# Causal attention, then a cosine MLP, on one core: other PSUM banks and another order for a few instructions

## The chip, the cores and the metric

One core of a Trainium2 chip. The core's engines are TensorE (PE; PEld is its weight load), VectorE (DVE), ScalarE (ACT), GpSimd (POOL) and SyncE (SP), which issues transfers. Each runs its own instructions in order and waits for the others by semaphores. PSUM has 8 banks, numbered 0 to 7 here. The metric is the device time of one execution in microseconds (us), the median of the runs.

## What is computed

Attention over 4 batches and 12 heads, 448 rows of 64, then an MLP of 768 to 2048 to 768 over 1792 tokens:

```python
scores = scale * np.matmul(q, k.transpose(0, 1, 3, 2))
scores = np.where(mask, -1000000000.0, scores)      # causal
attn = softmax(scores)
x = np.matmul(attn, v)        # laid out as 1792 tokens x 768
h = x @ w_in
out = (h * np.cos(h)) @ w_out
```

Inputs are float32; the two weight matrices come as float64 and are converted in the kernel.

## The kernel before

The order of all instructions is the order in which the code is written (a manual schedule); nothing reorders it. The program has two parts.

**Attention** (`attention`, the loop at L497) goes over N = 24 pairs of heads (4 batches by 6), one pair per step i, and works on several pairs at once, in a pipeline of steps. The 448 rows of a pair are three blocks of 128 and an end of 64; the causal mask leaves block rows 0, 1 and 2 ("top" is row 2, 384 wide; "low" are rows 0 and 1) and the end rows, which are done for two pairs together in odd steps. In step i:

- TensorE computes the scores of pair i (L336: top into banks 4 and 5, low into banks 6 and 7, the two heads j = 0 and 1 in one bank each), in odd steps the end scores of pairs i - 1 and i (L348, into banks 2 and 3), transposes the next pair's Q (L304, L307, bank 1), transposes the probabilities of pair i - 1 in three groups (`tp_top`, `tp_first`, `tp_last`, all at L422), transposes the next K (L304, bank 1 again), the end probabilities of pair i - 2 (`tp_ends`, L442), and forms P V of pair i - 3 (`av`, L457, bank 0).
- DVE masks the scores and takes the row maximum while it moves them out of PSUM (L357), forms the reciprocals of the sums (`inverse`, L389 and L390), copies the groups `tp_top` and `tp_first` out of PSUM (L311), and finishes P V (L479).
- ACT does the exponentials with their sums (L376) and the other copies out of PSUM (L313: Q, K, `tp_last`, and the ends in `evac_ends`), and the first half of finishing P V (L475).
- POOL multiplies the probabilities by the reciprocals (L396: low rows 0 and 1, ends, top), which must be done before they are transposed.

Between steps a piece of the MLP's first weights is converted (`convert_weight`: L128, L131, L137, L141 on DVE, L134, L142, L143 on POOL). Which bank a group of transposes uses is set in each step by the tuple `tb`:

```python
tb = (4, (TA_BANK, 6)[i % 2], 5, (6, 7)[i % 2])   # top, first, last, ends; TA_BANK = 2
```

so in even steps `tp_first` uses bank 2 and `tp_ends` bank 6, in odd steps 6 and 7. The next step's scores need banks 4 to 7 again, and its end scores banks 2 and 3. In steps N and N + 1 the first matmuls of the MLP (L589 to L591) fill TensorE's time (`fill`, banks 1 and 6).

**MLP** (`moe`) goes through slots k; each forms 2 x 18 matmuls of the first layer (L589 to L591, banks 4 and 5), the cosine of the result (`cosine_stages`: L597, L601, L602 on ACT, L599, L604 on DVE), and four chunks of the second layer for the slot before (`m2a_chunk`, L685, bank pairs 6-7 and 0-1 in turn), which DVE adds to the sums (L673). Between these the weights of later slots are converted: `mask` (L151, L153, L155 on ACT), `pack` (L162, L166, L170 on DVE), `halve` (L706 on ACT, L707 on POOL). `some(gen, n)` issues the next n stages of such a sequence, `run(gen)` the rest. The slots' code is `slot` at L879.

Of the kernel before, what the change touches and what calls it, by code (L numbers as in the profile page):

```python
# [21 lines left out]
def kernel(  # L22
# [19 lines left out]
    P = 128  # L42
# [55 lines left out]
    def f32(ap):  # L98
        return ap.bitcast(F32)
# [113 lines left out]
    def attention(filler_of):  # L213
        with (
# [94 lines left out]
            def evac(dst, src, dve=False):  # L309
                if dve:  # L310
                    nc.vector.tensor_copy(dst, src)  # L311
                else:
                    nc.scalar.copy(dst, src)  # L313

            def evac_qk(i, which, dve=False, n=W):
                d, s = qkt[i, which]
                evac(d[:, 0:n], s[:, 0:n], dve)
# [63 lines left out]
            def exp_block(i, c, j):  # L381
                exp(prob[i][:, j, OFF[c] : OFF[c] + (c + 1) * P], stats[i], col(c, j))
# [4 lines left out]
            def inverse(i, lo, up):  # L387
                st = stats[i]
                nc.vector.tensor_scalar(st[:, 2, lo:up], st[:, 1, lo:up], 1e-9, None, op0=ALU.add)  # L389
                nc.vector.reciprocal(st[:, 2, lo:up], st[:, 2, lo:up])  # L390
# [55 lines left out]
            def evac_ends(i, b):  # L446
# [2 lines left out]
                    banks8[:, b].rearrange("p (k h t) -> p k h t", k=NB + 1, h=2),  # L449
                )  # L450

            def av(i):
                vn, vt = vals.pop(i)
                o = banks8[:, O]
                for kc in range(NB + 1):
                    for j in range(2):
                        nc.tensor.matmul(  # L457
                            o[heads(j), kc * P : S],
                            lhsT=(vn[:, kc] if kc < NB else vt)[:, heads(j)],
                            rhs=ptr[i][:, j ^ i % 2, kc * (KS + P) : kc * KS + S],  # L460
                            start=(kc == 0), stop=(kc == NB),
                        )
                return o

            def x_of(i):
                b, hp = pairs[i]
# [5 lines left out]

            def finish_hi(i):
                for hi, _, cs in x_of(i):
                    nc.scalar.copy(hi, banks8[:, O, cs])  # L475

            def finish_lo(i):
                for hi, lo, cs in x_of(i):
                    nc.vector.tensor_tensor(lo, banks8[:, O, cs], f32(hi), op=ALU.subtract)  # L479

            extra = []

# [14 lines left out]
            for i in range(N + 4):  # L497
                cur, prev, nxt = i < N, 0 < i <= N, i + 1 < N
                ends_of, old, done = 0 <= i - 2 < N, 0 <= i - 3 < N, 0 <= i - 4 < N
                tb = (4, (TA_BANK, 6)[i % 2], 5, (6, 7)[i % 2])  # L500
                if i + 2 < N:
                    load_qk(i + 2)
                if prev:
                    load_v(i - 1)
                if i <= N:
                    open_stat(i)
                if cur:
                    open_scores(i)
                    scores_main(i, TOP, SC[0:2])
                    scores_main(i, LOW, SC[2:4])  # L510
                    if i % 2:
                        scores_ends(i - 1)
                if i == 0:
                    transpose_ends(0, O)
                    transpose_main(1, 1, TB_BANK)
                    transpose_main(1, 0, QK)
                    transpose_ends(1, QK)
                elif nxt:
                    transpose_main(i + 1, 0, QK)
                    transpose_ends(i + 1, QK)  # L520
                if done:
                    finish_hi(i - 4)
                if i == 1:
                    for j in range(2):
                        masked_block(i, 2, j, 0, SC[j])
                if 0 < i <= N + 1:
                    inverse(i - 1, 0 if prev else TAIL_COL, TAIL_COL + (i > 1))
                if prev:
                    normalise_block(i - 1, 0)
                    normalise_block(i - 1, 1)  # L530
                if ends_of:
                    normalise_ends(i - 2)
                if cur:
                    for j in range(2):
                        if i != 1:
                            masked_block(i, 2, j, 0, SC[j])
                        exp_block(i, 2, j)
                        if i and nxt and j == i % 2:
                            evac_qk(i + 1, 0, n=W + P)
                    if i == 0:  # L540
                        evac(qkt[0, 0][0][:, W : W + P], banks8[:, O, W : W + P])
                    masked_block(i, 0, 0, 0, SC[2])
                    if i == 0:
                        evac_qk(1, 1, dve=True)
                        evac_qk(1, 0, n=W + P)
                    masked_block(i, 1, 0, P, SC[2])
                if done:
                    finish_lo(i - 4)
                if cur:
                    inverse(i, TOP_COL, TOP_COL + 2)  # L550
                    normalise_block(i, 2)
                    masked_block(i, 0, 1, 0, SC[3])
                    masked_block(i, 1, 1, P, SC[3])
                    exp_block(i, 0, 0)
                    exp_block(i, 1, 0)
                if prev:
                    masked_ends(i - 1)
                if i in (N, N + 1):
                    fill((14, 12)[i - N])
                if prev:  # L560
                    open_ptr(i - 1)
                    tp_top(i - 1, tb[0])
                    tp_first(i - 1, tb[1])
                if prev:
                    tp_last(i - 1, tb[2])
                if nxt and i:
                    transpose_main(i + 1, 1, QK)
                    evac_qk(i + 1, 1)
                if cur:
                    exp_block(i, 0, 1)  # L570
                    exp_block(i, 1, 1)
                if prev:
                    exp_ends(i - 1)
                if ends_of:
                    tp_ends(i - 2, tb[3])
                    evac_ends(i - 2, tb[3])
                if i == N + 2:
                    run(extra[0])
                if old:
                    av(i - 3)  # L580
                yield i
# [71 lines left out]
    def some(gen, k=1):  # L653
        for _ in range(k):
            next(gen, None)

    def moe(ring, early, firsts):
        pend = None
        with tc.tile_pool(name="mo", bufs=1) as mo:
# [219 lines left out]
            def slot(g, t0, n, k, prev, first):  # L879
# [36 lines left out]
                if k in (2, 3):  # L916
                    run(pack(ia, mo))
                    some(firsts)
                    c0 = cosine_stages(hv[0], n)
                    some(c0, 2)  # L920
                    x_side(k - 3)
                    mb = mask(ib)
                    if k == 2:
                        some(mb)
                        some(c0)
                        side_out()
                    else:
                        some(c0)
                        some(mb)
                    some(mb)  # L930
                    (r0,) = c0
                    run(mb)
                    last_side()
                    ta = halve(ia)
                    run(m1_sum(ring, g, 1, t0, n, hv[1]))
                    pb = pack(ib, mo)
                    some(pb)
                    c1 = cosine_stages(hv[1], n)
                    some(c1)
                    if k == 2:  # L940
                        side_out()
                    gs.append(split(r0, *g_tiles(n)))
                    m2a_chunk(*prev, 0)
                    if k == 2:
                        some(c1)
                        some(pb)
                        some(c1)
                        m2a_chunk(*prev, 1)
                        run(pb)
                        tb = halve(ib)  # L950
                    else:
                        run(pb)
                        m2a_chunk(*prev, 1)
                        tb = halve(ib)
                        some(c1, 2)
                    if k == 2:
                        side_out()
                    mc = mask(ic)
                    some(mc)
                    (r1,) = c1  # L960
                    gs.append(split(r1, *g_tiles(n)))
                    if k == 3:
                        first_side(2, ta, tb)
                    m2a_chunk(*prev, 2)
                    run(mc)
                    m2a_chunk(*prev, 3)
                    if k == 2:
                        side_out()
                    store_side()
                    return gs  # L970
# [455 lines left out]
```

## Time and profile before

| what | value |
|---|---|
| median of 3 runs | 626.55 us (626.45 to 626.62) |
| profiled execution | 627.32 us, span 625.5 us |
| TensorE busy | 609.8 us (97% of the span) |
| DVE, ACT, POOL busy | 476.1, 419.5, 449.3 us |
| granted TensorE clock | 0.999 of full speed |
| moved by DMA | 133.27 MB, 212 GB/s over the span |

The attention takes about the first 180 us. Busy time of one engine says little by itself; what counts is who ends last at each place, which the waits and the order in time tell. A row of the order in time gives the start, the duration, the engine, the line and operation, the tiles with the number of instructions (x), and in brackets the idle time of the engine ahead of it and what ended it. A row of several instructions covers them from the first start to the last end. TensorE's matmuls overlap and their ends are modelled, so its idle time is better taken from start to start.

### The profile page before, as it was taken

Reading aid. Unit: us, or ns where it says so; the run is one execution under the profiler, and the core shown is the slowest. Engines: PE = TensorE matmul, PEld = TensorE weight load, DVE = VectorE, ACT = ScalarE, POOL = GpSimd, SP = SyncE. Lnnn points to the kernel's source line nnn. Section 1 sums busy time; section 2 is a strip of 40 time slices with the busy share of each in tenths; the row PEclk is TensorE's granted clock in tenths of the full one; section 3 lists DMA queues with packets and bytes.
Section 4 is the critical chain, followed back from the end, with each engine's and each line's share of the span. In section 5 each row is a group of like instructions: output and inputs, shape, how many; then the busy total and the mean of one; then the engine's idle time right before and its main releaser. Section 6 shows DMA issues by size and latency. Waiting matters only on the chain.

```text
span 625.5 us, 11531 instructions
## 1 busy us (share of the span) xinstructions
PE 609.8 (97%) x3825; PEld 537.2 (86%) x3825; DVE 476.1 (76%) x1023; ACT 419.5 (67%) x928; POOL 449.3 (72%) x456
## 2 busy tenths in 40 slices
PE   8799999999999999999999999999999999999996
PEld 6577667677669988999999999999999999999995
DVE  6788888888838678878777777764368887887886
ACT  5889988989766769877777777743335544644540
POOL 3676677677624968887877787772588788888885
PEclk9999999999999999999999999999999999999999
DMA  7656457563405776968696979669997568549104
GB/s 179 148 121 166 115 131 176 135 171 93 135 8 175 241 286 228 360 214 329 225 334 208 327 233 341 209 249 377 401 399 256 176 210 281 195 153 326 55 1 151
DMA packets 124042, 133.27 MB, mean 213 GB/s; under 512 B 72112, under 2 KB 108320, under 8 KB 123984
## 3 DMA queue, kind: packets, MB, share of 16 engines
q1 hardware_dynamic: 116384, 106.23, 53.8%
q0 software_dynamic: 4928, 24.78, 10.8%
q10 hardware_dynamic: 2672, 1.54, 0.8%
q8 instruction: 30, 0.49, 0.3%
q14 instruction: 28, 0.23, 0.1%
HBM read 82.58 MB, written 49.94 MB: 212 GB/s over the span
## 4 chain that ended last, share of the span: by engine, by line
PE 59%; DVE 2%; ACT 1%; issue 0%; DVEq 0%; ACTq 0%
PE banks L685 17%; PE banks L1113 12%; PE banks L1133 12%; PE banks L590 5%; PE banks L591 5%; PE banks L589 5%; PE banks L1037 2%; PE banks L1150 2%; DVE ct L170 0%; DVE acc L1160 0%; DVE banks L166 0%; DVE banks L162 0%; DVE r L599 0%; DVE acc L673 0%; DVE sct L770 0%
## 5 line engine op out<-in xcount | busy, mean ns | idle before, releaser
L673 DVE TENSOR_TENSOR acc<-acc,banks 128x768 f32<-128x768 f32 (+1 forms) x122 | 112.6, 932 | 43.2 <-PE banks L685 32.8
L685 PE MATMUL banks<-w,gh 128*128 128x384 f32 x512 | 109.8, 335 | 0.6 <-DVE acc L673 0.6
L685 PEld LDWEIGHTS banks<-w,gh 128*128 128x128 f32 x512 | 90.8, 188 | 2.4 <-DVE acc L673 1.3
L396 POOL TENSOR_TENSOR pb<-pb,stat 128x768 f32<-128x768 f32 (+2 forms) x72 | 74.0, 1042 | 24.9 <-DVE stat L390 10.1
L376 ACT ACTIVATE pb<-pb,stat 128x384 f32<-128x384 f32 (+1 forms) x144 | 72.1, 504 | 13.4 <-DVE stat L357 13.4
L591 PE MATMUL banks<-xa,w 128*128 128x512 f32 x192 | 75.2, 392 | 0.0
L590 PE MATMUL banks<-xa,w 128*128 128x512 f32 x192 | 75.0, 391 | 0.0
L589 PE MATMUL banks<-xa,w 128*128 128x512 f32 x192 | 74.9, 390 | 0.0
L707 POOL TENSOR_TENSOR w<-ct,w 128x768 fp32r<-128x768 f32 x28 | 51.9, 1854 | 19.0 <-PE banks L685 7.8
L685 PE MATMUL banks<-w,gl 128*128 128x384 f32 x256 | 65.1, 335 | 0.0
L357 DVE CUSTOM_DVE_ANT_0 pb<-banks,mask 128x384 f32<-128x384 f32 (+1 forms) x144 | 53.9, 418 | 7.9 <-PE banks L336 7.6
L597 ACT ACTIVATE ni<-banks 128x512 int32<-128x512 f32 (+1 forms) x64 | 34.5, 539 | 36.6 <-PE banks L591 22.7
L616 POOL TENSOR_TENSOR gl<-r,gh 128x512 fp32r<-128x512 f32 x32 | 41.5, 1300 | 20.4 <-ACT gh L615 20.2
L599 DVE SCALAR_TENSOR_TENSOR r<-ni,banks 128x512 f32<-128x512 int32 (+1 forms) x56 | 35.1, 626 | 21.5 <-ACT ni L597 21.0
L601 ACT ACTIVATE r<-r 128x512 f32<-128x512 f32 (+1 forms) x56 | 32.8, 586 | 23.0 <-DVE r L599 22.5
L336 PE MATMUL banks<-flat 64*128 64x256 f32 (+2 forms) x288 | 40.7, 402 | 6.2 <-ACT pm L313 3.2
L685 PEld LDWEIGHTS banks<-w,gl 128*128 128x128 f32 x256 | 46.4, 188 | 0.0
L604 DVE SCALAR_TENSOR_TENSOR r<-r,banks 128x512 f32<-128x512 f32 (+1 forms) x56 | 35.1, 626 | 14.0 <-ACT r L602 13.9
L1113 PE MATMUL banks<-xb,bb 128*128 128x384 f32 x234 | 44.7, 334 | 0.0
L457 PE MATMUL banks<-pm,vn 128*64 128x192 f32 (+2 forms) x288 | 44.1, 441 | 0.7 <-DVE xb L479 0.7
L1133 PE MATMUL banks<-big,gh 128*128 128x384 f32 x168 | 42.6, 334 | 0.0
L591 PEld LDWEIGHTS banks<-xa,w 128*128 128x128 f32 x192 | 36.0, 188 | 7.6
(149 smaller groups left out, 1528.2 us busy)
## 6 DMA issues: line engine op xcount, KB each, us to landing
bb<-w_in_d SPq DMA_DIRECT2D x48, 384.0 KB, 5.5
land<-in_moe_w_in_dram SPq DMA_DIRECT2D x14, 768.0 KB, 5.5
land<-in_moe_w_out_dram SPq DMA_DIRECT2D x14, 768.0 KB, 5.8
w_out_d<-w POOLq DMA_DIRECT2D x14, 768.0 KB, 5.2
big<-w_out_d SPq DMA_DIRECT2D x25, 384.0 KB, 4.0
w_in_d<-w POOLq DMA_DIRECT2D x7, 768.0 KB, 3.9
raw_d<-ct POOLq DMA_DIRECT2D x14, 384.0 KB, 7.8
land<-in_q_dram SPq DMA_DIRECT2D x48, 96.0 KB, 3.1
```

The costliest lines, as they stand in the source:

```text
L357: nc.vector.tensor_tensor_reduce(out=dst, in0=src, in1=m, scale=-scale, scalar=3.0e38, op0=ALU.add, op1=ALU.min, accum_out=st[:, 0, n : n ...
L376: nc.scalar.activation(dst, dst, AF.Exp, scale=-1.0, bias=st[:, 0, n : n + 1], accum_out=st[:, 1, n : n + 1],)
L396: nc.gpsimd.tensor_tensor(dst, dst, r.to_broadcast(list(dst.shape)), op=ALU.mult)
L457: nc.tensor.matmul(o[heads(j), kc * P : S], lhsT=(vn[:, kc] if kc < NB else vt)[:, heads(j)], rhs=ptr[i][:, j ^ i % 2, kc * (KS + P) : kc ...
L589: yield nc.tensor.matmul(hv, lhsT=wh[:, f], rhs=x[:, 0, cc, t], start=(cc == 0), stop=False)
L590: yield nc.tensor.matmul(hv, lhsT=wh[:, f], rhs=x[:, 1, cc, t], start=False, stop=False)
L591: yield nc.tensor.matmul(hv, lhsT=wl[:, f], rhs=x[:, 0, cc, t], start=False, stop=(cc == NCC - 1))
L673: nc.vector.tensor_tensor(d, d, o, op=ALU.subtract)
L685: nc.tensor.matmul(o[:, e, 0:EH], lhsT=a[:, cs], rhs=w[:, e * EH : (e + 1) * EH], start=(x == 0), stop=(x == 5),)
L707: nc.gpsimd.tensor_tensor(w[:, 1], tf, f32(w[:, 0]), op=ALU.subtract)
L1113: nc.tensor.matmul(o, lhsT=w[:, u, k * P : (k + 1) * P], rhs=x[k][:, v], start=k + m == 0, stop=k == K - 1 and m == 2,)
L1133: nc.tensor.matmul(o[:, b % 2, 0:EH], lhsT=g_ops[i][u][:, c * P : (c + 1) * P], rhs=wouts[g, i][:, v], start=(x == 0), stop=(x == 2),)
```

## The change

Five edits; no instruction is added or taken away.

1. Banks and order of the transposes: `tp_top` in bank 4, then `tp_last` in 5, then `tp_first` in 6, in every step; `tp_ends` in bank 2 in even steps, 7 in odd ones.
2. In every step the reciprocal of the top sums (`inverse` of 2 columns) and the top normalisation behind it come after the low masked rows of the second head instead of before.
3. Steps 0 to 2: in step 0 the copy of the next Q moves between the two top exponentials; in step 1 the transposes and the copy of the next K move ahead of two exponentials and of `tp_last` and `tp_first`; in step 2 the top masked rows move ahead of the reciprocals, as in step 1.
4. P V of the last pair goes to bank 7 instead of bank 0.
5. In slot 3 the first mask stage comes ahead of the cosine's ACT stages, and one more `pack` stage ahead of the first chunk.

```diff
--- before.py
+++ after.py
@@ -449,9 +449,12 @@
                     banks8[:, b].rearrange("p (k h t) -> p k h t", k=NB + 1, h=2),
                 )
 
+            def o_of(i):
+                return banks8[:, 7 if i == N - 1 else O]
+
             def av(i):
                 vn, vt = vals.pop(i)
-                o = banks8[:, O]
+                o = o_of(i)
                 for kc in range(NB + 1):
                     for j in range(2):
                         nc.tensor.matmul(
@@ -460,7 +463,6 @@
                             rhs=ptr[i][:, j ^ i % 2, kc * (KS + P) : kc * KS + S],
                             start=(kc == 0), stop=(kc == NB),
                         )
-                return o
 
             def x_of(i):
                 b, hp = pairs[i]
@@ -472,11 +474,11 @@
 
             def finish_hi(i):
                 for hi, _, cs in x_of(i):
-                    nc.scalar.copy(hi, banks8[:, O, cs])
+                    nc.scalar.copy(hi, o_of(i)[:, cs])
 
             def finish_lo(i):
                 for hi, lo, cs in x_of(i):
-                    nc.vector.tensor_tensor(lo, banks8[:, O, cs], f32(hi), op=ALU.subtract)
+                    nc.vector.tensor_tensor(lo, o_of(i)[:, cs], f32(hi), op=ALU.subtract)
 
             extra = []
 
@@ -497,7 +499,7 @@
             for i in range(N + 4):
                 cur, prev, nxt = i < N, 0 < i <= N, i + 1 < N
                 ends_of, old, done = 0 <= i - 2 < N, 0 <= i - 3 < N, 0 <= i - 4 < N
-                tb = (4, (TA_BANK, 6)[i % 2], 5, (6, 7)[i % 2])
+                e_bank = (TA_BANK, 7)[i % 2]
                 if i + 2 < N:
                     load_qk(i + 2)
                 if prev:
@@ -520,7 +522,7 @@
                     transpose_ends(i + 1, QK)
                 if done:
                     finish_hi(i - 4)
-                if i == 1:
+                if i in (1, 2):
                     for j in range(2):
                         masked_block(i, 2, j, 0, SC[j])
                 if 0 < i <= N + 1:
@@ -532,38 +534,42 @@
                     normalise_ends(i - 2)
                 if cur:
                     for j in range(2):
-                        if i != 1:
+                        if i not in (1, 2):
                             masked_block(i, 2, j, 0, SC[j])
                         exp_block(i, 2, j)
-                        if i and nxt and j == i % 2:
+                        if nxt and j == i % 2:
                             evac_qk(i + 1, 0, n=W + P)
-                    if i == 0:
-                        evac(qkt[0, 0][0][:, W : W + P], banks8[:, O, W : W + P])
                     masked_block(i, 0, 0, 0, SC[2])
                     if i == 0:
                         evac_qk(1, 1, dve=True)
-                        evac_qk(1, 0, n=W + P)
+                        evac(qkt[0, 0][0][:, W : W + P], banks8[:, O, W : W + P])
                     masked_block(i, 1, 0, P, SC[2])
                 if done:
                     finish_lo(i - 4)
                 if cur:
+                    masked_block(i, 0, 1, 0, SC[3])
+                    masked_block(i, 1, 1, P, SC[3])
                     inverse(i, TOP_COL, TOP_COL + 2)
                     normalise_block(i, 2)
-                    masked_block(i, 0, 1, 0, SC[3])
-                    masked_block(i, 1, 1, P, SC[3])
-                    exp_block(i, 0, 0)
-                    exp_block(i, 1, 0)
+                    if i != 1:
+                        exp_block(i, 0, 0)
+                        exp_block(i, 1, 0)
                 if prev:
                     masked_ends(i - 1)
                 if i in (N, N + 1):
                     fill((14, 12)[i - N])
                 if prev:
                     open_ptr(i - 1)
-                    tp_top(i - 1, tb[0])
-                    tp_first(i - 1, tb[1])
+                    tp_top(i - 1, 4)
+                if i == 1:
+                    transpose_main(i + 1, 1, QK)
+                    evac_qk(i + 1, 1)
+                    exp_block(i, 0, 0)
+                    exp_block(i, 1, 0)
                 if prev:
-                    tp_last(i - 1, tb[2])
-                if nxt and i:
+                    tp_last(i - 1, 5)
+                    tp_first(i - 1, 6)
+                if nxt and i > 1:
                     transpose_main(i + 1, 1, QK)
                     evac_qk(i + 1, 1)
                 if cur:
@@ -572,8 +578,8 @@
                 if prev:
                     exp_ends(i - 1)
                 if ends_of:
-                    tp_ends(i - 2, tb[3])
-                    evac_ends(i - 2, tb[3])
+                    tp_ends(i - 2, e_bank)
+                    evac_ends(i - 2, e_bank)
                 if i == N + 2:
                     run(extra[0])
                 if old:
@@ -920,13 +926,10 @@
                     some(c0, 2)
                     x_side(k - 3)
                     mb = mask(ib)
+                    some(mb)
+                    some(c0)
                     if k == 2:
-                        some(mb)
-                        some(c0)
                         side_out()
-                    else:
-                        some(c0)
-                        some(mb)
                     some(mb)
                     (r0,) = c0
                     run(mb)
@@ -940,6 +943,8 @@
                     if k == 2:
                         side_out()
                     gs.append(split(r0, *g_tiles(n)))
+                    if k == 3:
+                        some(pb)
                     m2a_chunk(*prev, 0)
                     if k == 2:
                         some(c1)
```

Banks don't show in an instruction's row below, which names all of PSUM `banks`. Three places in the order of the instructions show the rest.

DVE, the middle of step 5 (`xa<-banks,xa` finishes P V of an earlier pair; `pb` are probabilities, `stat` the sums), before:

```order
L479 TENSOR_TENSOR xa<-banks,xa 128x448
L389 TENSOR_SCALAR stat<-stat 128x2
L390 RECIPROCAL stat<-stat 128x2
L357 ISA pb,stat<-banks,mask 128x128
L357 ISA stat 128x1
L357 ISA pb,stat<-banks,mask 128x256
L357 ISA stat 128x1
L357 ISA pl_94,stat<-banks,mask_t 128x448
```

and now:

```order
L481 TENSOR_TENSOR xa<-banks,xa 128x448
L357 ISA pb,stat<-banks,mask 128x128
L357 ISA stat 128x1
L357 ISA pb,stat<-banks,mask 128x256
L357 ISA stat 128x1
L389 TENSOR_SCALAR stat<-stat 128x2
L390 RECIPROCAL stat<-stat 128x2
L357 ISA pl_94,stat<-banks,mask_t 128x448
```

The two rows of the reciprocal moved behind the two masked rows, and so behind nothing else; it is the same in every step.

ACT in slot 3 (`r` is the cosine's argument, `flat` the mask's buffer, `land` the raw weights), before:

```order
L597 ACTIVATE ni<-banks 128x512
L601 ACTIVATE r<-r 128x512
L602 ACTIVATE r<-r 128x512
L151 ACTIVATE flat<-land,flat 128x768
L153 ACTIVATE flat<-flat 128x768
L155 ACTIVATE banks<-flat 128x2x384
```

and now (L603, L607 and L608 are the old L597, L601 and L602):

```order
L603 ACTIVATE ni<-banks 128x512
L151 ACTIVATE flat<-land,flat 128x768
L607 ACTIVATE r<-r 128x512
L608 ACTIVATE r<-r 128x512
L153 ACTIVATE flat<-flat 128x768
L155 ACTIVATE banks<-flat 128x2x384
```

The mask's first stage moved ahead of the two cosine stages.

DVE in slot 3 (`acc` are the second layer's sums), before:

```order
L162 SCALAR_TENSOR_TENSOR banks<-land,banks 128x2x384
L673 TENSOR_TENSOR acc<-acc,banks 128x768
L166 SCALAR_TENSOR_TENSOR banks<-land,banks 128x2x384
L170 SCALAR_TENSOR_TENSOR ct<-land,banks 128x768
L673 TENSOR_TENSOR acc<-acc,banks 128x768
```

and now (L679 is the old L673):

```order
L162 SCALAR_TENSOR_TENSOR banks<-land,banks 128x2x384
L166 SCALAR_TENSOR_TENSOR banks<-land,banks 128x2x384
L679 TENSOR_TENSOR acc<-acc,banks 128x768
L170 SCALAR_TENSOR_TENSOR ct<-land,banks 128x768
L679 TENSOR_TENSOR acc<-acc,banks 128x768
```

The second `pack` stage moved ahead of the first addition.

## Rows read from the trace of the kernel before

**Rows 1.** Waits of PE: line, releaser, us in total, times, longest.

```profile
PE banks L336 <- ACT pm L313: 3.2, 11, 0.5
...
PE banks L336 <- ACT flat L313: 1.6, 2, 0.9
```

**Rows 2.** Busy us (instructions) by stretch, then granted clock, DMA share, GB/s.

```profile
100.00:150.00 50.00, 48.92 (x440) 35.12 (x439) 44.32 (x183) 44.83 (x147) 35.62 (x42) 1.00 0.62 151
...
300.00:400.00 100.00, 100.00 (x509) 91.31 (x509) 76.10 (x96) 76.50 (x116) 78.45 (x74) 1.00 0.81 276
```

**Rows 3.** PE in order of time, an even and an odd step.

```profile
98.51 1.57 PE L336 MATMUL banks<-flat 64*128 64x384 f32 x12
100.01 0.55 PE L304 MATMUL banks<-ident,land 128*128 128x128 f32 x3
...
104.55 0.92 PE L336 MATMUL banks<-flat 64*128 64x384 f32 x4
...
105.74 0.93 PE L336 MATMUL banks<-flat 64*128 64x128 f32 x8 [0.27 <-ACT pm L313]
...
106.59 0.99 PE L348 MATMUL banks<-flat 64*64 64x384 f32 x16
...
108.01 1.47 PE L422 MATMUL banks<-ident,pb 128*128 128x128 f32 x12
...
112.05 1.57 PE L336 MATMUL banks<-flat 64*128 64x384 f32 x12
```

**Rows 4.** ACT in order of time, the same odd step.

```profile
105.11 0.57 ACT L313 COPY pm<-banks 128x512 f32<-128x512 f32 x1
...
108.21 0.59 ACT L313 COPY flat<-banks 128x512 f32<-128x512 f32 x1 [0.56 <-PE banks L307]
```

**Rows 5.** DVE in order of time, the same two steps.

```profile
98.55 0.17 DVE L389 TENSOR_SCALAR stat<-stat 128x5 f32<-128x5 f32 x1 [0.59 <-ACT pl L376]
...
99.57 0.56 DVE L357 CUSTOM_DVE_ANT_0 pb<-banks,mask 128x384 f32<-128x384 f32 x1 [0.62 <-PE banks L336]
...
101.98 0.17 DVE L389 TENSOR_SCALAR stat<-stat 128x2 f32<-128x2 f32 x1 [0.28 <-ACT pb L376]
...
105.07 0.42 DVE L141 SCALAR_TENSOR_TENSOR ct<-st,ct 128x256 f32<-128x256 f32 x1
...
107.90 0.47 DVE L389 TENSOR_SCALAR stat<-stat 128x2 f32<-128x2 f32 x1
```

**Rows 6.** POOL in order of time, the same two steps.

```profile
100.66 0.94 POOL L396 TENSOR_TENSOR pl<-pl,stat 128x448 f32<-128x448 f32 x1
...
105.56 0.40 POOL L142 CAST w<-ct 128x256 fp32r<-128x256 f32 x1 [1.57 <-DVE ct L141]
...
106.73 1.61 POOL L396 TENSOR_TENSOR pb<-pb,stat 128x256 f32<-128x256 f32 x2
108.30 0.94 POOL L396 TENSOR_TENSOR pl<-pl,stat 128x448 f32<-128x448 f32 x1
```

**Rows 7.** PE in order of time, steps 2 and 3.

```profile
16.46 1.57 PE L336 MATMUL banks<-flat 64*128 64x384 f32 x12 [0.73 <-ACT flat L313]
...
23.07 0.92 PE L336 MATMUL banks<-flat 64*128 64x384 f32 x4 [1.26 <-DVE pm L311]
24.47 0.93 PE L336 MATMUL banks<-flat 64*128 64x128 f32 x8 [0.49 <-ACT pm L313]
```

**Rows 8.** ACT and PE at P V of the last pair.

```profile
179.00 0.58 ACT L313 COPY pm<-banks 128x512 f32<-128x512 f32 x1
...
181.47 1.84 PE L457 MATMUL banks<-pm,vn 128*64 128x448 f32 x12 [0.66 <-DVE xb L479]
```

**Rows 9.** PE, ACT and DVE in order of time, slots 3 and 4.

```profile
231.41 0.96 PE L685 MATMUL banks<-w,gh 128*128 128x384 f32 x4 [0.20 <-DVE acc L673]
...
246.60 0.97 PE L685 MATMUL banks<-w,gh 128*128 128x384 f32 x4 [0.43 <-DVE acc L673]
...
222.72 0.63 ACT L601 ACTIVATE r<-r 128x512 f32<-128x512 f32 x1 [1.23 <-DVE r L599]
...
226.75 0.96 DVE L162 SCALAR_TENSOR_TENSOR banks<-land,banks 128x768 uint32<-128x768 uint32 x1 [2.02 <-ACT banks L155]
```

## Prediction

> **What bounds the kernel now.** I read the list of TensorE's waits first [rows 1], then busy time by stretch [rows 2]. TensorE is the engine that ends last nearly everywhere: in the stretch 300 to 400 us of the MLP it is busy 100.00 of 100 us, so there only its own work counts, and whatever arrives there earlier leaves earlier. In the stretch 100 to 150 us of the attention it is busy 48.92 of 50, VectorE (DVE) 44.32, ScalarE (ACT) 44.83, GpSimd (POOL) 35.62. No transfer is among TensorE's waits. So a gain can come from TensorE's waits alone, and the largest entry is L336 (scores) waiting for ACT's evacuations, 11 times.
>
> The order in time of TensorE over one pair of steps, even then odd [rows 3], shows that wait. An even step issues its scores from 98.51 to 100.01 in one piece, 1.50. The odd step issues the two top rows at 104.55 and the eight low ones only at 105.74. Low rows take 106.59 - 105.74 = 0.85, so top rows cost 1.50 - 0.85 = 0.65, and the odd step lost 105.74 - 104.55 - 0.65 = 0.54. (The 0.27 of idle in the row is smaller, because it counts from a modelled end.) What released it is ACT's copy of the end rows out of bank 6, 105.11 + 0.57 = 105.68 [rows 4]. A pair takes 112.05 - 98.51 = 13.54; without the wait TensorE needs 13.00.
>
> **Part 1: banks.** In even steps the transposes of the end rows go to bank 2 instead of 6, and the first blocks go to bank 6 instead of 2. Bank 6 is then released by DVE's second transpose copy, which ends before DVE's next conversion, the last of which starts at 105.07 [rows 5]; the low scores could start at 104.55 + 0.65 = 105.20, so this wait goes: -0.54 per odd step. What is late next? Bank 2 is now written by ACT's late copy's source, and the scores of the ends want it at 104.55 + 1.50 = 106.05; ACT frees it at 105.68. That holds by 0.37.
>
> The next thing is POOL. The transposes of an odd step would start at 108.01 - 0.54 = 107.47, and their second group at about 107.47 + 4 x 0.12 = 107.95 (twelve take 1.47 [rows 3]). In the new order the second group is the "last" blocks, whose first block needs POOL's second normalisation at once; the group that stood there before needs it two transposes later. POOL ends it at 106.73 + 1.61 = 108.34 [rows 6]: 0.4 too late, unless POOL comes earlier too.
>
> **Part 2: reciprocal later.** DVE waits 0.28 for ACT before L389 in the even step and now does two masked rows first, which are ready. The wait goes, and DVE, which has no other wait up to there, reaches the conversion L141 about 0.3 earlier, by 104.8 instead of 105.07. POOL's chain hangs on it: POOL's first conversion row starts 105.56, 0.49 behind L141 [rows 5, 6], and POOL then runs through without a gap. So POOL's second normalisation ends at about 108.0 (108.34 - 0.3), and with 0.06 for the signal TensorE waits 0.1 instead of 0.4. Net per odd step: 0.54 - 0.1 = 0.43 (0.09 if POOL doesn't move, 0.54 if it moves far enough).
>
> The same edit has a price in the odd step. There L389 took 0.47 at 107.90, where it takes 0.17 elsewhere, and it ended at 108.37, 0.03 behind POOL's L396, which ended at 108.34 [rows 5, 6]. So a DVE row that should be short was held for 0.3 until a POOL instruction was through. Moved back by the two earlier waits, and held up by two masked rows more, it comes at about 108.2 at the latest, just when POOL has begun the next L396 (108.30 - 0.3, for 0.94, so to 108.9): a hold of 0.65. Behind it on DVE are the masked end rows and both transpose copies. I cost this at nothing: DVE idles 0.59 before L389 and 0.62 before L357 at the even step [rows 5], 1.2 a pair. The shorter pair takes 0.43 of it, the longer hold 0.35, and what is left covers it.
> The Trainium skill ("SBUF — State Buffer", section "SBUF: two separate sides") calls the port pair of VectorE and GpSimd an exclusive lock that the first comer holds for a whole instruction; by that rule the later place costs nearly one whole L396, not a share of it. The row agrees (0.47 ending right behind POOL). By the rule the sum stays as it is while the slack holds; where it doesn't, it is the last rival below.
>
> In the even step POOL's L396 of the ends stops at 100.66 + 0.94 = 101.60 [rows 6], and L389 would come no earlier than where it stood, 101.98, and by my count at 102.2, behind the two masked rows: not held, with some 0.5 to spare.
>
> **Part 3: steps 0 to 3.** TensorE's waits there are 0.73 at 16.46 for ACT, 1.26 at 23.07 for DVE, 0.49 at 24.47 for ACT [rows 7]; with the other wait for ACT (1.6 for the two [rows 1]) that is 3.4 at most. In step 0 the 512-wide copy moves ahead of an exponential, so step 1's scores start 0.2 earlier, but ACT stands half a microsecond until TensorE has transposed, and its exponentials, and POOL behind them, come 0.4 to 0.6 later. In step 1 the copy of K moves ahead of two exponentials, so K is there a microsecond earlier, but the copy that frees bank 5 moves behind both, and step 2's second score row must wait for it, to about 16.9. I book nothing for steps 0 to 2 (bounds -0.6 and +1.6). In step 2 the later reciprocal brings DVE's first transpose copy forward by 0.5, so step 3 starts about 0.8 earlier (23.07 to 22.3); the scores of the ends then wait for ACT's copy, now out of bank 2, until 24.5, where they used to start 0.85 behind 24.47. Taken together 0.8 by step 4, with step 3's own 0.54 in it.
>
> **Part 4: own bank for the last P V.** L457 at 181.47 waits 0.66 for DVE's L479 [rows 8], that is for bank 0. Bank 7 is free once ACT's copy at 179.00 has ended, 0.58 later. Gone: 0.66 as shown, some 0.8 from start to start.
>
> **Part 5: slot three.** L685 waits 0.20 at 231.41 and 0.43 at 246.60 for DVE's additions [rows 9]; 0.63 in all, and some 0.9 from start to start, since the idle time of a matmul counts from a modelled end (as in rows 3, 0.27 for 0.54). ACT stood 1.23 before L601 at 222.72, and the mask row (L151, about 1.0) now fits into that gap. So DVE's L162, which waited 2.02 for ACT's L155, comes 1.0 earlier (226.75 to 225.7), L166 goes before the first addition, and the chain of ACT and DVE that ends at 246.60 follows one microsecond earlier. The first addition of slot three is not later, since it waits for TensorE anyhow. Both waits go: 0.9.
>
> **The sum.** Steps 0 to 3: 0.8. Ten odd steps, 5 to 23, at 0.43: 4.3. Last P V 0.8, slot three 0.9. Together 6.8. The profiled execution took 627.32 (span 625.5, 1.8 around it), 0.77 above the median of the runs shown, 626.55. 627.32 - 6.8 = 620.5, and at the level of the median 619.8.
>
> **Rivals.**
> More: the POOL wait vanishes and steps 0 to 2 give too: 11 x 0.54 + 1 to 1.6 + 1.7 = 8.6 to 9.2, so 617.4 to 618. For it: the 0.1 left is small. Against: the new order of the groups brings the need for POOL forward.
> POOL takes the place: DVE's saved 0.3 does not reach L141, TensorE waits 0.45 in each odd step, and 0.09 is left: 10 x 0.09 + 0.35 + 1.7 = 3.0, so 623.6. For it: POOL runs gapless from 105.56 to 109.24. Against: nothing on DVE between the reciprocal and L141 waits for another engine.
> Nothing (within 0.2%, about what a measurement of this kernel can tell from no change): the odd steps give nothing, steps 0 to 2 lose 0.6 and the chain in slot three is as late as before: 0.8 for the last P V less 0.6, so 626.4.
> Slower: the hold of L389 moves into the even step. If POOL's normalisation of the ends there runs past 102.2, 0.6 later than now, L389 is held up to 0.94 more, and L141, POOL's conversion and both normalisations of the odd step follow one for one. POOL would end at 108.34 - 0.3 + 0.94 = 109.0, TensorE would wait 1.0 instead of the 0.54 saved, and 11 x 0.47 = 5.2 would be lost against 1.7 + 0.3 gained: 629.7. For it: such a hold is in the trace. Against: in the even step POOL is done with the ends before L389 in the trace.
> The Trainium skill's page "SBUF — State Buffer" (section "SBUF: two separate sides") has the rule that would make that hold a whole instruction long.
>
> **Chances.** My forecast 0.60 (618.4 to 621.2), more 0.14, POOL takes the place 0.14, nothing 0.06, slower 0.06. Faster 0.88, same 0.06, slower 0.06. The range 617.4 to 623.3 takes in the forecast, most of "more" and half of the POOL case, and leaves out some 0.2.
>
> **What would show it.** In the new trace a pair of steps takes 13.1; an odd step's twelve scores run in one piece of 1.5; between the first and the second group of transposes in odd steps is a wait for POOL's L396 of about 0.1; L389 of the odd step lasts 0.6 to 0.9 and the one of the even step 0.17 without idle time before it; no wait before the last P V nor in the two slots. I am wrong if the pair stays above 13.4, if DVE has no idle time left at the start of even steps, or if L348 waits for bank 2.

## The result and the profile after

The changed kernel took 620.73 us (620.15 to 620.90) beside 626.50 for the kernel before on the same chip: ratio 0.9906, 95% interval 0.9889 to 0.9923, so 5.9 us less (4.8 to 7.0). The predicted time was 619.8, the range 617.4 to 623.3. The profiled execution took 620.15 with a span of 618.0.

TensorE's waits of the kernel after, as in [rows 1] (line, releaser, us in total, times, longest):

```profile
PE banks L422 <- POOL pb L396: 1.7, 3, 1.1
...
PE banks L336 <- ACT flat L313: 0.7, 1, 0.7
PE banks L304 <- ACT flat L313: 0.7, 1, 0.7
PE banks L348 <- ACT pm L313: 0.4, 1, 0.4
```

and one line of the waits of its weight loads (PEld):

```profile
PEld banks L422 <- POOL pb L396: 4.6, 13, 1.4
```

The eleven waits of the scores (L336) for ACT's copy out of bank 6 are gone; waits for POOL stand first now: 1.13 in step 2, 0.17 in step 7, 0.38 in step 23. The ordinary odd step is missing from TensorE's own list, since idle time counts from a modelled end; it is in that of the weight loads, and its length is read from starts. A usual pair of steps, 12 and 13 ([rows 3] shows 14 and 15, which take the same time before), in order of time (start, duration, line, tiles, number):

```profile
88.35 1.57 PE L336 MATMUL banks<-flat 64*128 64x384 f32 x12
89.85 0.99 PE L348 MATMUL banks<-flat 64*64 64x384 f32 x16
90.77 0.55 PE L304 MATMUL banks<-ident,land 128*128 128x128 f32 x3
91.16 0.27 PE L307 MATMUL banks<-ident,land 128*128 128x128 f32 x1
91.26 1.65 PE L422 MATMUL banks<-ident,pb 128*128 128x128 f32 x12
...
91.81 0.86 PEld L422 LDWEIGHTS banks<-ident,pb 128*128 128x128 f32 x8 [0.19 <-POOL pb L396]
...
92.75 0.49 PE L304 MATMUL banks<-ident,land 128*128 128x128 f32 x3
...
95.48 1.57 PE L336 MATMUL banks<-flat 64*128 64x384 f32 x12
```

The odd step's twelve scores run in one piece, 89.85 - 88.35 = 1.50, and the scores of the ends (L348) follow without a wait. The twelve transposes take 92.75 - 91.26 = 1.49 from start to start where they took 1.31, so 0.18 is lost inside that row. The weight loads show where: the second group starts at 91.81, 0.55 behind the first instead of 4 x 1.31 / 12 = 0.44, and 0.05 behind the end of POOL's second normalisation (91.76, below). So 0.11 of it is the wait for POOL; the other 0.07 is lost behind the wait, where the last eight take 0.94 instead of 0.87. The even step's scores started at 82.31, so this pair takes 13.17. Of the nine pairs from step 4 on five take 13.17 to 13.19, one (42.57 to 55.96) 13.39, and the last three 13.26 or 13.27; all were 13.54 or 13.55.

DVE and POOL in the same two steps, to be read like [rows 5] and [rows 6]:

```profile
88.49 0.42 DVE L141 SCALAR_TENSOR_TENSOR ct<-st,ct 128x256 f32<-128x256 f32 x1
...
92.16 0.51 DVE L389 TENSOR_SCALAR stat<-stat 128x2 f32<-128x2 f32 x1
92.71 0.17 DVE L390 RECIPROCAL stat<-stat 128x2 f32<-128x2 f32 x1
...
96.54 0.56 DVE L357 CUSTOM_DVE_ANT_0 pb<-banks,mask 128x384 f32<-128x384 f32 x1 [0.80 <-PE banks L336]
```

```profile
90.14 1.62 POOL L396 TENSOR_TENSOR pb<-pb,stat 128x256 f32<-128x256 f32 x2
91.71 0.94 POOL L396 TENSOR_TENSOR pl<-pl,stat 128x448 f32<-128x448 f32 x1
```

L141 comes 88.49 - 82.31 = 6.18 behind the even step's scores (before: 105.07 - 98.51 = 6.56), so 0.38 earlier. POOL's second normalisation ends at 91.76, 9.45 behind them (before 9.83): the same 0.38.

Where the time went, by TensorE's starts in the two traces:

| stretch | before | after | gain | predicted |
|---|---|---|---|---|
| scores of step 0 to scores of step 4 | 23.87 | 23.27 | 0.60 | 0.8 |
| scores of step 4 to the last P V | 150.68 | 146.74 | 3.94 | 4.3 + 0.8 |
| last P V to the last matmul | 437.65 | 436.67 | 0.98 | 0.9 |
| together | 612.20 | 606.68 | 5.52 | 6.8 |

The spans differ by 7.5. The other 2.0 lie outside this chain: step 0's scores start 0.80 earlier (over the traces of this study at 6.06 to 7.23, with no order by kernel, and the first loads come before them), and 1.2 lie behind the last matmul, where the trace of the kernel before has 6.4, that of edit 2 alone 5.7 and all others here 5.2. So kernels are compared below by **TensorE's chain**, from the first scores to the last matmul, beside the timed ratio; ratios are to the kernel before on the same chip. A pair is a usual one, of steps 10 to 15.

### The profile page after: what moved, and what is told of

The parts are those of the page before. It is cut to its first block, busy times and chain, and to the rows that moved or that the text cites. A ratio compares the mean times of both kernels' runs of the same rounds, so it can differ in the third digit from the quotient of the medians.

```text
span 618.0 us, 11520 instructions
## 1 busy us (share of the span) xinstructions
PE 607.7 (98%) x3825; PEld 536.7 (87%) x3825; DVE 479.7 (78%) x1023; ACT 419.4 (68%) x928; POOL 448.9 (73%) x456
## 4 chain that ended last, share of the span: by engine, by line
PE 94%; ACT 2%; DVE 2%; POOL 1%; issue 1%; DVEq 0%; POOLq 0%
PE banks L691 22%; PE banks L1118 12%; PE banks L1138 12%; PE banks L597 7%; PE banks L595 7%; PE banks L596 7%; PE banks L460 7%; PE banks L336 5%; PE banks L422 5%; PE banks L304 3%; PE banks L1042 2%; PE banks L442 1%; PE banks L348 1%; PE banks L1155 1%; ACT pb L376 1%; POOL pb L396 1%
## 5 line engine op out<-in xcount | busy, mean ns | idle before, releaser
L679 DVE TENSOR_TENSOR acc<-acc,banks 128x768 f32<-128x768 f32 (+1 forms) x122 | 112.6, 932 | 43.9 <-PE banks L691 33.5
L597 PE MATMUL banks<-xa,w 128*128 128x512 f32 x192 | 75.2, 392 | 0.0
L603 ACT ACTIVATE ni<-banks 128x512 int32<-128x512 f32 (+1 forms) x64 | 34.5, 538 | 36.6 <-PE banks L597 22.6
L607 ACT ACTIVATE r<-r 128x512 f32<-128x512 f32 (+1 forms) x56 | 32.8, 586 | 21.9 <-DVE r L605 21.4
L597 PEld LDWEIGHTS banks<-xa,w 128*128 128x128 f32 x192 | 36.0, 188 | 7.6
L595 PEld LDWEIGHTS banks<-xa,w 128*128 128x128 f32 x192 | 36.1, 188 | 7.2
```

Of the source, the lines that this page charges most:

```text
L595: yield nc.tensor.matmul(hv, lhsT=wh[:, f], rhs=x[:, 0, cc, t], start=(cc == 0), stop=False)
L597: yield nc.tensor.matmul(hv, lhsT=wl[:, f], rhs=x[:, 0, cc, t], start=False, stop=(cc == NCC - 1))
L679: nc.vector.tensor_tensor(d, d, o, op=ALU.subtract)
```

## The experiments

| kernel | median us | ratio (95%) | chain us | pair us |
|---|---|---|---|---|
| before | 626.50 | 1 | 612.20 | 13.54 |
| after | 620.73 | 0.9906 (0.9889 to 0.9923) | 606.68 | 13.18 |
| edit 1 alone | 626.60 | 0.9991 (0.9981 to 1.0001) | 613.08 | 13.55 |
| edit 2 alone | 626.23 | 0.9996 (0.9982 to 1.0010) | 612.14 | 13.54 |
| after without edit 2 | 624.62 | 0.9960 (0.9947 to 0.9972) | 610.80 | 13.55 |
| after without edit 3 | 620.71 | 0.9906 (0.9893 to 0.9919) | 607.02 | 13.18 |
| after without edits 4, 5 | 622.26 | 0.9926 (0.9914 to 0.9939) | 608.09 | 13.18 |
| after, old order of groups | 622.25 | 0.9930 (0.9916 to 0.9944) | 608.13 | 13.40 |
| after, row 1 normalised first | 618.73 | 0.9864 (0.9847 to 0.9882) | 604.82 | 13.00 |
| after, no addition in the reciprocal | 617.97 | 0.9858 (0.9845 to 0.9872) | 604.37 | 13.01 |
| both of these | 617.46 | 0.9847 (0.9829 to 0.9865) | 603.79 | 13.00 |
| before, no addition | 625.54 | 0.9976 (0.9965 to 0.9987) | 611.47 | 13.54 |

### Are banks and reciprocal two gains, or one?

Theory: the banks take one wait away and put another of the same length, for POOL, in its place; the later reciprocal shortens that one. Rival: each has its own gain. Edit 1 alone (in the kernel before):

```diff
-                tb = (4, (TA_BANK, 6)[i % 2], 5, (6, 7)[i % 2])
+                e_bank = (TA_BANK, 7)[i % 2]
...
-                    tp_top(i - 1, tb[0])
-                    tp_first(i - 1, tb[1])
-                if prev:
-                    tp_last(i - 1, tb[2])
+                    tp_top(i - 1, 4)
+                    tp_last(i - 1, 5)
+                    tp_first(i - 1, 6)
...
-                    tp_ends(i - 2, tb[3])
-                    evac_ends(i - 2, tb[3])
+                    tp_ends(i - 2, e_bank)
+                    evac_ends(i - 2, e_bank)
```

> The kernel before with edit 1 alone (banks and order of the transposes). Theory: the wait for ACT's copy in the odd step goes, and the second group of transposes waits for POOL's second normalisation instead, about as long: the kernel after shows 0.17 there with DVE's L141 0.38 earlier, so without that 0.17 + 0.38 = 0.55 against the 0.54 saved. Time 626.2 to 626.6, pair of steps 13.5. Rival (the edits simply add up, and the reciprocal's place does not matter): ten odd steps at 0.32, so 623.3, pair 13.2.

TensorE in an odd step of this kernel:

```profile
91.38 1.57 PE L336 MATMUL banks<-flat 64*128 64x384 f32 x12
92.88 0.99 PE L348 MATMUL banks<-flat 64*64 64x384 f32 x16
...
94.30 0.60 PE L422 MATMUL banks<-ident,pb 128*128 128x128 f32 x4
95.23 1.09 PE L422 MATMUL banks<-ident,pb 128*128 128x128 f32 x8 [0.33 <-POOL pb L396]
```

The wait for bank 6 is gone, and the second group starts 0.93 behind the first instead of 0.44: 0.49 lost there, and 0.06 more up to the next L304: 0.55 for the 0.54 saved. Nothing is gained in time either, as the theory had it.

Edit 2 alone (the same four lines, exchanged, in the kernel before):

```diff
-                    inverse(i, TOP_COL, TOP_COL + 2)
-                    normalise_block(i, 2)
                     masked_block(i, 0, 1, 0, SC[3])
                     masked_block(i, 1, 1, P, SC[3])
+                    inverse(i, TOP_COL, TOP_COL + 2)
+                    normalise_block(i, 2)
```

> The kernel before with edit 2 alone (reciprocal of the top sums after the low masked rows). Theory: TensorE still waits 0.54 per odd step for ACT's copy out of bank 6, which does not hang on DVE or POOL; 626.0 to 626.6, and POOL's normalisations end 0.3 to 0.4 earlier without use. Rival (DVE's place is what gives the time): 623.5 or less.

TensorE and POOL there, scores of the even step at 97.93:

```profile
97.93 1.57 PE L336 MATMUL banks<-flat 64*128 64x384 f32 x12
...
105.15 0.93 PE L336 MATMUL banks<-flat 64*128 64x128 f32 x8 [0.27 <-ACT pm L313]
```

```profile
105.78 1.61 POOL L396 TENSOR_TENSOR pb<-pb,stat 128x256 f32<-128x256 f32 x2
```

POOL ends at 107.39, 9.46 behind the scores instead of 9.83, and TensorE still waits for ACT's copy: 0.37 that nobody uses, and no gain in time. The kernel after with edit 2 undone:

> The kernel after with edit 2 undone. Theory: the wait for POOL in odd steps grows from 0.17 to about 0.55, ten times 0.38, so 620.7 + 3.8 = 624.5, and up to 0.5 more from steps 2 and 3. Rival (the later place only moves L389 behind POOL, where it is held, and costs as much as it gives): 620.7 or less.

Measured 624.62, where the theory had 624.5, and a chain 4.1 longer; the pair is back at 13.55, with the wait for POOL at 0.33 in the list again (0.55 from start to start). All three say the same: **neither edit gives anything alone, and together they give 0.36 a pair.** The rival of the prediction in which POOL takes the place of the wait is what the kernels with edit 1 and without edit 2 show; with both edits POOL is 0.38 earlier, and the change escapes it. Edit 1 undone in the kernel after was not run; edit 2 alone stands for it in these steps.

### What is left of the wait for POOL, and who sets it

Row 1 normalised before row 0, since the second group needs row 1 alone:

```diff
-                    normalise_block(i - 1, 0)
                     normalise_block(i - 1, 1)
+                    normalise_block(i - 1, 0)
```

> The kernel after, with POOL's two low normalisations in the other order (row 1 before row 0), since the second group of transposes needs row 1 alone. Theory: row 1 is then there 0.57 earlier, the wait of 0.17 in ten odd steps goes (0.38 in two of them), and part of the 1.13 in step 2: 1.7 + 0.4 + 0.5 = 2.6, so 618.1, pair 13.0. Rival: the third group, which now needs what POOL ends last, or DVE's copies behind it, take the place of the wait: 620.7.

A pair of steps of it:

```profile
81.93 1.57 PE L336 MATMUL banks<-flat 64*128 64x384 f32 x12
...
90.89 1.47 PE L422 MATMUL banks<-ident,pb 128*128 128x128 f32 x12
...
94.93 1.57 PE L336 MATMUL banks<-flat 64*128 64x384 f32 x12
```

The transposes are back at 1.47 and the pair at 13.00, the time that the prediction gave TensorE without any wait. In step 2 the wait for POOL falls from 1.13 to 0.56, but steps 0 to 4 gain only 0.30 by it. The chain is 1.86 shorter than after's, the ratio 0.0042 lower, and the two intervals do not meet; 0.38 of what the attention gained is lost again behind the last P V. So what was missing from the sum sat in this wait: with it all 0.18 go, its 0.11 and the 0.07 behind it.

The reciprocal without the addition of 1e-9 (the sums are 1 or more):

```diff
-                nc.vector.tensor_scalar(st[:, 2, lo:up], st[:, 1, lo:up], 1e-9, None, op0=ALU.add)
-                nc.vector.reciprocal(st[:, 2, lo:up], st[:, 2, lo:up])
+                nc.vector.reciprocal(st[:, 2, lo:up], st[:, 1, lo:up])
```

> The kernel after without L389 (the addition of 1e-9 to the sums, which are 1 or more), reciprocals taken from the sums directly. It tests the held row: DVE has 0.17 and, where POOL's normalisation stands ahead, 0.36 to 0.51 less. Theory: L141 comes 0.2 earlier, POOL's second normalisation with it, the wait of 0.17 in the odd steps goes: 13.0 a pair, 618.9. The reciprocal, which moves to the place of L389, is held in its stead where POOL works on: 0.5 instead of 0.17 in odd steps. Rival for the hold: only the addition is held, and the reciprocal takes 0.17 to 0.19 everywhere. Rival for the time: POOL is not released by L141 earlier, pair 13.18, 620.7.

DVE and POOL, odd step (lines are one lower, L389 is now the reciprocal):

```profile
91.17 0.16 DVE L389 RECIPROCAL stat<-stat 128x2 f32<-128x2 f32 x1
```

```profile
90.68 0.94 POOL L395 TENSOR_TENSOR pl<-pl,stat 128x448 f32<-128x448 f32 x1
```

The pair is 13.01, as the theory had it, and the time 0.9 less than expected. For the hold the rival was right: the reciprocal starts and ends in the middle of POOL's row (90.68 to 91.62) and takes 0.16. Only the addition is held.

Both together:

> The kernel after with both finds: row 1 normalised before row 0, and the reciprocal without the addition. Theory: TensorE ran without a gap from step 4 on with either, at 13.0 a pair, so the two don't add up there; what is left to gain is in the waits of steps 2 and 3 for POOL (0.56 and 0.88 alone) and in the last steps: 0.3 to 0.6 below 618.0, so 617.4 to 617.7. Rival (what the addition costs is a sum of its own, beside the wait): 2.0 + 2.76 = 4.8 below 620.7, so 616.0.

617.46, and the chain 0.58 shorter than with the addition's removal alone: no sum of two gains, since both take away the same wait. It is the fastest kernel here, 9.6 us under the kernel before. And the addition taken out of the kernel before:

> The kernel before without the addition L389. The same cut that gave 2.76 in the kernel after. Theory: in the kernel before TensorE waits in the odd steps for ACT's copy out of bank 6, which hangs neither on DVE nor on POOL; so only steps 1 to 3 can gain: 0 to 0.6, 625.9 to 626.5. Rival (DVE's 0.34 to 0.64 a step count whatever TensorE waits for): 2.7 or more, 623.8.

The pair stays at 13.54 and the scores still wait for ACT. Scores of step 0 to step 4 are 0.50 shorter, as expected; the chain 0.73. The timed gain, 0.0024 or 1.5 us (0.8 to 2.2), is more than the 0.6 of my theory and less than the rival's 2.7; the rest lies outside the chain and is not explained. The same cut took 2.31 off the chain of the kernel after.

### Banks apart from order

The kernel after with `tp_first` again ahead of `tp_last` (banks 6 and 5 kept):

```diff
-                    tp_last(i - 1, 5)
                     tp_first(i - 1, 6)
+                    tp_last(i - 1, 5)
```

> The kernel after with the new banks but the old order of the groups (top, first, last). It parts banks from order within edit 1. Theory: the second group then needs POOL's row 1 two transposes (0.22) later, which is past the 0.17: no wait for POOL, pair 13.0, 618.9; so the new order has cost 0.17 per odd step. Rival: ACT's copy of the last group, 0.44 later, is late for the next scores in bank 5: an odd or even step waits 0.2 or more there, and the time is 620.7 or above.

Neither came whole. The odd step lost its wait for POOL, as I expected, but the even step got a new one, and the time is 622.25 (TensorE, then DVE, even step):

```profile
85.14 0.60 PE L422 MATMUL banks<-ident,pb 128*128 128x128 f32 x4
85.94 1.06 PE L422 MATMUL banks<-ident,pb 128*128 128x128 f32 x8 [0.21 <-DVE stat L357]
```

```profile
85.37 0.42 DVE L357 CUSTOM_DVE_ANT_0 pb<-banks,mask 128x256 f32<-128x256 f32 x1
85.71 0.08 DVE L357 DVE_READ_ACCUMULATOR2_ANT stat<- 128x1 f32 x1
```

In an even step no end scores stand between scores and transposes, and DVE has only just masked the low rows out of bank 6 when the second group wants to write there: 85.94 - 85.14 = 0.80 instead of 0.44. The pair is 13.40. So the new order is what makes bank 6 usable in even steps; it costs 0.18 in odd ones and saves 0.4 in even ones. My rival had the right side of the time and the wrong bank and engine.

### Edits 3, 4 and 5

> The kernel after with edit 3 undone (steps 0 to 2 in the old order). Theory: edit 3 does little by itself, since what steps 2 and 3 gained comes from banks and reciprocal: scores(0) to scores(4) 23.3 to 23.9 where the kernel after has 23.27, so 620.7 to 621.3. Rival: all of the 0.6 gained in steps 0 to 3 and more comes from it: scores(0) to scores(4) 24.1 as with edit 1 alone, 621.6.

Steps 0 to 4 take 29.82 - 6.26 = 23.56 without edit 3 and 23.27 with it; the timed ratio is the same, 0.9906, as the theory had it. Edit 3 is worth 0.3 in the trace and nothing that a measurement shows.

Edits 4 and 5 undone (`o_of` returns bank 0 always; slot three's `some(mb)`, `some(c0)` and `some(pb)` in the old order):

> The kernel after with edits 4 and 5 undone (last P V in bank 0, old order in slot three). Theory: the wait of 0.66 before the last P V and the two in slot three come back, 0.74 and 0.97 from start to start: 620.7 + 1.7 = 622.4. Rival: with TensorE 3.8 earlier at the end of the attention DVE's finishing rows stand otherwise and the waits are smaller than in the kernel before: 621.0 or less.

TensorE at the last P V and in slots 3 and 4 of this kernel:

```profile
177.69 1.84 PE L460 MATMUL banks<-pm,vn 128*64 128x448 f32 x12 [0.36 <-DVE xb L481]
...
227.62 0.98 PE L691 MATMUL banks<-w,gh 128*128 128x384 f32 x4 [0.22 <-DVE acc L679]
...
242.80 0.98 PE L691 MATMUL banks<-w,gh 128*128 128x384 f32 x4 [0.42 <-DVE acc L679]
```

All three waits of [rows 8] and [rows 9] are back, the first smaller, and the time is within 0.2 of the 622.4 expected. From the last four matmuls (`vt`) of the P V before it to the last P V lie 177.69 - 174.54 = 3.15 here, 2.71 in the kernel after, 3.45 in the kernel before: edit 4 is worth 0.44, and 0.30 of the 0.74 gained there came from the other edits. The chain is 1.41 longer; behind the last P V it is 0.96.

## Why the prediction was right, point by point

**The bound.** TensorE's waits alone could give time, and did. In the stretch 300 to 400 us it is busy 100.00 in both kernels [rows 2]; in 100 to 150 it went from 48.92 to 49.89:

```profile
100.00:150.00 50.00, 49.89 (x450) 35.06 (x446) 45.37 (x178) 45.64 (x149) 36.66 (x43) 1.00 0.56 138
300.00:400.00 100.00, 100.00 (x509) 91.22 (x508) 76.80 (x97) 76.61 (x116) 78.43 (x74) 1.00 0.81 276
```

**Part 1.** The wait for bank 6 went and POOL stood next in line, as worked out. The claim that L348 holds by 0.37 for bank 2 is right from step 5 on; the one wait of 0.43 is in step 3, as foretold.

**Part 2.** The 0.3 saved on DVE did reach POOL one for one (0.38), which was what parted the forecast from its rival. **The mis-sized term is the ten odd steps**: 4.3 predicted, about 3.2 measured. Predicted was 0.54 less a new wait of 0.1. The wait itself came out at 0.11, but with luck: I took 0.12 for the pitch of the transposes, where it is 1.31 / 12 = 0.109, so the second group wants to start 0.44 behind the first and not 0.48, and my own numbers (108.34 - 0.3 + 0.06 - 107.95) give 0.15 before rounding; POOL coming 0.38 earlier instead of 0.3 made up for that. What the sum put at nothing is what is lost behind a wait, 0.07 here and 0.06 with edit 1 alone; why was not tested. So 0.18 is lost in all, and 0.36 is left of 0.43. Five of the ten gained that.

In the last three pairs POOL's second normalisation ended 9.54 behind the even step's scores instead of 9.45, and 0.28 was left. There the columns of a pair lie over two tiles, and DVE finishes P V in two rows instead of the one of 0.62 (step 18):

```profile
124.51 0.29 DVE L481 TENSOR_TENSOR xa<-banks,xa 128x128 fp32r<-128x128 f32 x1
124.71 0.48 DVE L481 TENSOR_TENSOR xb<-banks,xb 128x320 fp32r<-128x320 f32 x1
```

The next row starts 125.11 - 124.51 = 0.60 behind them instead of 0.54, which is most of the 0.09. In the kernel before it cost nothing, since the reciprocal there waited 0.28 for ACT anyway [rows 5].

Two odd steps waited longer still. In step 23 no next Q is transposed, so the groups come 0.49 earlier. In step 7 the pair kept only 0.15: the normalisation ahead of POOL's conversion began 4.55 behind the even step's scores instead of 4.19, and while POOL was at it (until 48.59) DVE's L137 took longer than its usual 0.41:

```profile
47.12 1.47 POOL L396 TENSOR_TENSOR pb<-pb,stat 128x768 f32<-128x768 f32 x1 [1.55 <-DVE stat L357]
```

```profile
48.24 0.63 DVE L137 SCALAR_TENSOR_TENSOR ct<-st,ct 128x256 uint32<-128x256 uint32 x1
```

The normalisation is as late in step 6 of the kernel before (48.71, 4.38 behind the scores, 4.02 in step 8) and of every kernel here that has the addition ahead of the reciprocal, and in none of the three without it; why stays open.

**The hold.** L389 of the odd step lasts 0.51 in the rows above, a hold of 0.34 where I had 0.65, and so falls short of the 0.6 to 0.9 that I named as a sign; it lasts 0.69 in the pair at 121.94 and 0.89 in step 7. In the usual pair it comes when POOL is already 92.16 - 91.71 = 0.45 into its row; I had it 0.2 in. It cost nothing, as booked: DVE idles 0.80 at the start of the even step. In the even step L389 takes 0.16 to 0.17 without idle time; the slower rival did not come. What I left out: the row for the sums at the head of the odd step (128x5) is held by POOL's L142 in six of the ten and takes 0.36 to 0.38 instead of 0.17, with no cost that shows.

**Part 3.** 0.8 booked for steps 0 to 4, 0.60 measured. I booked nothing for edit 3 itself, which gave 0.3; the two other edits alone gave 23.87 - 23.56 = 0.3 of the 0.8.

**Parts 4 and 5.** 0.8 and 0.9 booked, 0.74 and 0.98 measured. No wait stands before the last P V or in slot 3. In slot 4 the row that waited 0.43 carries no idle time, but follows 1.17 behind the four before it, and the next four follow 1.17 behind it, where 1.04 is usual: 0.26 is left of that wait, so "both waits go" was not quite true.

By the chain the sum was 1.3 too large, in time 0.9 (620.73 against 619.8).

## What to carry over

Moving a buffer gains only the time up to the next thing in line; work out that next one from the trace, and move it too, as here POOL, for which TensorE had not waited in these steps. Count a new wait with what is lost behind it: 0.11 cost 0.18 here. When two edits each give nothing, test them together, and test each undone, before dropping one. Then look at what is left (0.18 to 0.26 in most odd steps): exchanging two rows on the engine that sets it took 1.9 us off the chain, taking out a needless short row ahead of it 2.3.

## What the hardware showed beyond that

A DVE row that POOL holds up shows as a longer row, not as idle time or a wait. Step 7 of the kernel after has it at full length, DVE and POOL:

```profile
52.27 0.89 DVE L389 TENSOR_SCALAR stat<-stat 128x2 f32<-128x2 f32 x1
53.19 0.17 DVE L390 RECIPROCAL stat<-stat 128x2 f32<-128x2 f32 x1
```

```profile
52.20 0.93 POOL L396 TENSOR_TENSOR pl<-pl,stat 128x448 f32<-128x448 f32 x1
```

It ends at 53.16, 0.03 behind POOL's row, for work of 0.17. The Trainium skill ("SBUF — State Buffer", section "SBUF: two separate sides") has the port pair that VectorE and GpSimd share locked for a whole instruction by whichever starts first, a GpSimd instruction or a VectorE one in a two-port mode or with two inputs in SBUF; the other waits. The rows agree: DVE's row, which starts 0.07 behind POOL's, ends right behind it. The Trainium skill's page "VectorE: DVE Perf Modes" (section "Mode 2×_2P — use both read ports for one tensor") gives a two-port mode to scalar operations with a single tensor and to copies; it doesn't speak of the reciprocal there. The rows agree for the scalar operation: the addition of a constant is held. The reciprocal of the same 128x2 numbers, inside the same POOL row, is not (0.16).
